# Seven half products for the last 256 tokens, and weight sums and loads put in other queues

## Chip, cores and metric

The kernel runs on one core of one Trainium2 chip. The metric is the device time of one execution in microseconds, as the median of several runs. Before the change it is 205.13 us (three runs, 204.55 to 205.29).

TensorE (PE) multiplies matrices into PSUM, VectorE (DVE), ScalarE (ACT) and GpSimd (POOL) work element by element, and SyncE (SP) issues most of the DMAs. Each engine takes its instructions in the order in which the program lists them for it. They wait for one another through semaphores.

## The reference

The reference is a cross attention between tokens `x` (8 batches, 8 heads, 512 tokens, 64 wide) and a state of 32 tokens per head, followed by a two-layer network with SiLU:

```python
a = softmax(scale * x @ state.T);   xread = a @ state    # 512 tokens a batch
a2 = softmax(scale * state @ x.T);  sread = a2 @ x       # 32 tokens a batch
t = concatenate([xread, sread])     # heads side by side: 512 wide, 544 tokens a batch
h = t @ w_in                        # 512 -> 2048
out = (h * sigmoid(h)) @ w_out      # 2048 -> 512, float32
```

The 32 state-read tokens of all eight batches make 256 tokens, which the kernel treats as a ninth unit at the end.

## The kernel before the change

**Stages.** Batch 0 is written out by hand. Then comes a loop over batches b = 1 to 7 (line 858). For each, `emit_G1` (line 549) makes 16 tiles of 128 hidden features by 512 tokens: TensorE multiplies, ScalarE applies SiLU and writes the tile `g`. The attention of an x-read batch is folded into the weights: `W1[b]` (lines 462 to 493) is the state times `w_in`, and `aT[b]` holds the normalised weights of the attention. `upto(k)` (line 710) emits G1 tiles until k are done, so it places G1 work between other products. n = b + 1 and m = b + 2 name the batches prepared during batch b.

**Output product of a batch.** `class Unit` (line 608) does the output product in the manner of Strassen and Winograd: the 2048 features are cut in two halves of eight tiles, the 512 output columns in two halves of 256, and the 512 tokens in two halves of 256. Seven half products then stand in for eight. `mm` (line 623) numbers them 1 to 7. They need sums of the token tiles (`sums3`, `sums2`, `sums1`, `sums4`, on VectorE) and sums of weights, `D1` to `D4`, which `t_weights` (line 596) makes once. During batch 1, `D2` and `D4` are completed for their second half of the features by two VectorE sums (lines 936 and 972). Results are gathered in the two tiles `u.o[0]` and `u.o[1]` (tags `o_sb0` and `o_sb1`, one buffer each) and written by `out_half(1)` and `out_half(0)`.

**Order of the batch.** Within batch b the list is: G1 tiles from `lead` to 15 with products 1 and 7 between them (lines 884 to 912), then product 2, 6, 4, 5, 3 (lines 945 to 1009). At j = 5 the first `sums3` and, from batch 2 on, the next load of x; at j = 9 the second `sums3` and, in batches 1 and 2, `evict_state`, which places transposed states into `stT` (in batch 2 ahead of `norm_t`). In batch 1, lines 971 to 980 place `t_weights`, `spread_x`, the normalisation and transposes of batch 2's attention, `exps_t(m)` (it ends with a DMA transpose into `e`) and `fetch_x(m + 1)` (two loads of x of 512 KB each, from SyncE's queue). `cast_x` and `transpose_x` at the batch's end (lines 1010 to 1013) need that load.

**State-read tokens.** `emit_G1` makes 16 tiles of 256 tokens for them (lines 555 to 566), spread over batch 7's products. After batch 7, lines 1014 to 1022 do the output product directly: the first 128 tokens by 16 matmuls of 512 columns (`G2`, line 577), then `last_cols` (line 691) three times for the other 128 tokens: 256 columns, 128 and 128, 16 matmuls each, each followed by a copy to a buffer of its own and a DMA.

**Places that the change and the prediction touch.** `D2`, `D4` and `t_weights`: lines 586 to 606, 936, 972. `evict_state` in batch 2: line 903. `fetch_x` in batch 1: line 979. The sum that frees PSUM for product 3: line 989. `scores_t`, which reads `xT`: line 329. The tail: lines 1016 to 1022. Helpers: `copy` (160, 162), `sub` (591), `add` (594).

Of the kernel before, what the change touches and what calls it, by code (L numbers as in the profile page):

```python
# [8 lines left out]
FP32 = mybir.dt.float32  # L9
# [9 lines left out]
B = 8  # L19
# [23 lines left out]
def kernel(  # L43
# [33 lines left out]
    def bank(shape, dtype, name):  # L77
        tag = banks[turn[0] % len(banks)]
        turn[0] += 1
        return psA.tile(shape, dtype, tag=tag, name=name)  # L80
# [77 lines left out]
    def copy(eng, dst, src):  # L158
        if eng is nc.scalar:
            nc.scalar.activation(dst, src, func=COPY, bias=0.0)  # L160
        else:
            eng.tensor_copy(dst, src)  # L162
# [123 lines left out]
    def evict_state(u, eng, b0, nb):  # L286
        to = stT.rearrange("p b k s (n m v) -> p b k s n m v", n=2, m=8)
        for g in range(2):
            for v in range(2):
                copy(  # L290
                    eng,
                    to[ds(64 * u, 64), ds(b0, nb), ds(2 * g, 2), u ^ g, :, :, v],
                    st_x[
                        ds(64 * v, 64), :, ds(b0, nb), ds(2 * g, 2), u, :
                    ].rearrange("p m b k n -> p b k n m"),
                )
# [391 lines left out]
            nc.sync.dma_start(out_sread[ds(512, 32), ds(4 * tt, 4), :], o[:])  # L688


    def last_cols(b, tt, f, n, eng, queue):
        cols = ds(f, n)
        ps = bank([128, DM], FP32, "o_part")
        for ft in range(NFT):
            nc.tensor.matmul(  # L695
                ps[:, 0:n],
                gt[b * NFT + ft][:, ds(128 * tt, 128)],
                w_out_sb[:, ft, cols],
                start=(ft == 0),
                stop=(ft == NFT - 1),  # L700
                skip_group_check=True,
            )
        o = opool.tile([128, n], FP32, tag=f"o_part{f}", name="o_part")
        copy(eng, o[:], ps[:, 0:n])
        queue.dma_start(out_sread[ds(512, 32), ds(4 * tt, 4), cols], o[:])


    done = [0]

    def upto(k):  # L710
        while done[0] < min(k, (B + 1) * NFT):
            emit_G1(done[0])
            done[0] += 1
# [139 lines left out]
    def fetch_x(i):  # L853
        n = 4 if i < 6 else H
        for h in range(0, H, n):
            load_x(i, h, n, nc.sync)

    for b in range(1, B):
        n = b + 1
        m = n + 1  # L860
        u = Unit(b)
        lead = 3 if b == 1 else LEADS
        last = 6 if b == 1 else 8
        todo = [(1, k) for k in range(last)] + [(7, k) for k in range(8)]
        todo += [(1, k) for k in range(last, 8)]
        n_todo = len(todo)

        def unit():
            p, k = todo.pop(0)
            u.mm(p, k)  # L870
            if (p, k) == (1, 7):
                u.keep(nc.vector, 0, 0)
            if (p, k) == (7, 7):
                copy(nc.vector, u.block(1, 1), u.be[:])

        def early(j):
            while (
                todo
                and todo[0][1] + (0 if todo[0][0] == 1 else 2) <= j - 2
                and (n_todo - len(todo)) * (NFT - lead) < 16 * (j + 1 - lead)  # L880
            ):
                unit()

        for j in range(lead, NFT):
            upto(NFT * b + j + 1)
            if j == 8:
                u.hi = gh[b, 1]
            if j == max(lead, 5):
                if b == 1:
                    t_weights((3,), 4, 4)  # L890
                    transpose_x(3)
                u.sums3(0, 4)
                if 1 < b and m + 1 < B:
                    fetch_x(m + 1)
            if j == 9:
                u.sums3(4, 4)
                if b == 1:
                    for v in range(2):
                        evict_state(v, (nc.vector, nc.gpsimd)[v], 2, 2)
                elif n < B:  # L900
                    if b == 2:
                        for v in range(2):
                            evict_state(v, (nc.vector, nc.gpsimd)[v], 4, 4)
                    norm_t(n)
                    if b in SREAD_AT:
                        spread_x(n)
                else:
                    for half in range(2):
                        place_xm(half, nc.vector)
            early(j)  # L910
            if j == 13:
                u.sums2(0, 4)
        srs = SREAD_AT.get(b, ())

        def group_a():
            pss = w1_next(PIECES_A[b])
            if m < B:
                scores_t(m)
            ps_sr = sread(srs, bank if m < B else new_h) if srs else None
            return pss, ps_sr  # L920

        def out_a():
            w1_out(*made[0][0])
            if srs:
                sread_out(srs, made[1])
            for piece in made[0][1:]:
                w1_out(*piece)

        while todo:
            unit()  # L930
        u.sums2(4, 2)
        if 1 < b < B - 1:
            made = group_a()
        u.sums2(6, 2)
        if b == 1:
            t_weights((2,), 4, 4)
            u.sums1()
        if 1 < b < B - 1:
            out_a()
        if n == B:  # L940
            upto(NFT * B + 2)
        if b == 1:
            for hg in range(2):
                scores(2, hg)
        for k in range(8):
            u.mm(2, k)
        add(nc.vector, u.block(0, 0), u.block(0, 0), u.be[:])
        if b == 1:
            for hg in range(2):
                exps(2, hg)  # L950
        elif m < B:
            nc.scalar.activation(warm[:], busy[:, 0:1], func=EXP, bias=0.0)

        if 1 < b and m < B:
            exps_t(m)
        step = 0

        def units(p, leads={}):
            nonlocal step
            for k in range(8):  # L960
                u.mm(p, k)
                if n == B and (p != 6 or k > 5):
                    upto(NFT * B + 2 + (step + 1) * (NFT - 2) // 26)
                    step += 1
                if n < B and k in leads:
                    upto(NFT * n + leads[k])

        units(6)
        u.keep(nc.scalar, 1, 0)
        add(nc.gpsimd, u.block(1, 0), u.block(1, 0), u.block(1, 1))  # L970
        if b == 1:
            t_weights((4,), 4, 4)
            spread_x(2)
            for hg in range(2):
                norm(2, hg)
                transpose_a(2, hg)
            made = group_a()
            exps_t(m)
            fetch_x(m + 1)
            out_a()  # L980
        else:
            u.sums1()
            if n < B and b not in SREAD_AT:
                spread_x(n)
        if m < B:
            nc.scalar.activation(warm[:], busy[:, 0:1], func=SILU, bias=0.0)
        units(4)
        u.sums4()
        add(nc.vector, u.block(1, 0), u.block(1, 0), u.be[:])
        def group_b():  # L990
            if b in PIECES_B:
                c = PIECES_B[b]
                pss = w1_next(2) + (w1_next(1, new_h) if c == 3 else [])
                for i in (2, 0, 1)[3 - c :]:
                    if b == 1 and i == 1:
                        pss[i] = pss[i][:2] + ((nc.vector, nc.vector),) + pss[i][3:]
                    w1_out(*pss[i])

        if b > 1:
            group_b()  # L1000
        units(5, {7: 1} if b > 1 else {})
        u.keep(nc.scalar, 0, 1)
        add(nc.gpsimd, u.block(1, 1), u.block(1, 1), u.block(0, 1))
        u.out_half(1)
        if b == 1:
            group_b()
        units(3, {1: 2, 3: 3, 5: 4, 7: 5})
        add(nc.vector, u.block(0, 1), u.block(0, 1), u.be[:])
        u.out_half(0)
        if m + 1 < B:  # L1010
            for c in range(4):
                cast_x(m + 1, nc.gpsimd, c, 1)
            transpose_x(m + 1)
        for ft in range(NFT):
            gt.pop(NFT * b + ft)
    for ft in range(NFT):
        upto(NFT * B + ft + 2)
        G2(B, 0, ft)
    store(B, 0, nc.scalar)
    last_cols(B, 1, 0, 256, nc.scalar, nc.sync)  # L1020
    last_cols(B, 1, 256, 128, nc.vector, nc.scalar)
    last_cols(B, 1, 384, 128, nc.vector, nc.sync)
# [1 line left out]
_INS = ['x', 'state', 'moe_w_in', 'moe_w_out']  # L1024
_OUTS = [((4352, 512), 'float32')]
# [25 lines left out]
```

## Time and profile before

| what | value |
|---|---|
| median of three runs | 205.13 us |
| the profiled execution | 204.79 us |
| its span | 202.9 us |
| granted TensorE clock, mean | 0.998 |
| GpSimd busy | 68.2 us (34%) |
| DMA moved | 28.71 MB, mean 141 GB/s |

The span is the profiled part of the execution; 1.9 us lie around it. In a timeline row, the first figure is the start in us from the span's begin, the second the length of the group, then engine, line, operation, output and inputs with their shapes, and how many instructions were merged. Square brackets give the idle time of the engine ahead of the row and what ended it. That releaser is inferred: where several things were awaited, it is the one that came last by the profile, and a DMA can hide behind it. "PEld" is TensorE's loading of weights, which runs beside its matmuls. A DMA has two times: the length of its issue in a queue (SPq is SyncE's), and the time from the issue to its landing.

### The profile page before, as it was taken

How to read it: one execution, taken by the hardware profiler on the slowest of the kernel's cores; microseconds unless marked ns; L12 is line 12 of the kernel's file. 1: busy time of each engine (PE TensorE's matmuls, PEld its weight loads, DVE VectorE, ACT ScalarE, POOL GpSimd, SP SyncE). 2: the span in 40 equal slices, each digit the busy share in tenths (PEclk: the TensorE clock that was granted, in tenths of full speed). 3: DMA queues.
4: the chain of work that ended last, by engine and by line, in shares of the span. 5: the costliest groups of instructions: out<-in, count | busy, mean ns of one | idle time of the engine just before them, and what ended most of it. 6: DMA issues, size and time to landing. Idle time of an engine off the chain costs nothing.

```text
span 202.9 us, 4636 instructions
## 1 busy us (share of the span) xinstructions
PE 194.5 (96%) x1893; PEld 129.7 (64%) x1912; DVE 133.6 (66%) x237; ACT 137.5 (68%) x243; POOL 68.2 (34%) x87
## 2 busy tenths in 40 slices
PE   7799999999989989999999999999999999999993
PEld 2454445458756577667766677668766876688862
DVE  2852747958985999387947974779369955861101
ACT  2875667888767867889778957788588168724510
POOL 8682343850623703730373033332202230002200
PEclk9999999999999999999999999999999999999999
DMA  6999999992078992495229913944142005000222
GB/s 196 196 206 207 264 249 359 240 234 52 3 149 284 216 253 56 167 275 129 52 114 181 280 21 55 279 86 29 29 203 55 13 3 207 0 3 0 103 107 103
DMA packets 40965, 28.71 MB, mean 141 GB/s; under 512 B 27376, under 2 KB 37616, under 8 KB 40944
## 3 DMA queue, kind: packets, MB, share of 16 engines
q1 hardware_dynamic: 34736, 20.65, 39.9%
q0 software_dynamic: 5920, 7.64, 18.2%
q8 instruction: 15, 0.25, 0.5%
q10 hardware_dynamic: 288, 0.13, 0.3%
q14 instruction: 6, 0.05, 0.1%
HBM read 17.43 MB, written 8.91 MB: 130 GB/s over the span
## 4 chain that ended last, share of the span: by engine, by line
PE 87%; DVE 7%; DMA 2%; issue 1%; ACT 1%
PE o L642 40%; PE h L540 25%; PE o L577 5%; PE ps_w L473 4%; PE h L558 4%; PE o_a L577 3%; DMA x_f<-in_x_dram 2%; PE o_part L695 2%; DVE o_sb L162 1%; PE ps_xt L257 1%; PE ps_sr L420 1%; DVE s L591 1%; DVE g L591 1%; DVE W L162 1%; ACT xT L160 1%
## 5 line engine op out<-in xcount | busy, mean ns | idle before, releaser
L568 ACT ACTIVATE g<-h 128x512 bf16<-128x512 f32 (+1 forms) x142 | 79.9, 573 | 34.6 <-PE h L540 17.4
L642 PEld LDWEIGHTS <-g 128*128 128x128 bf16 x560 | 54.1, 98 | 30.2 <-issue 1.4
L540 PE MATMUL h<-aT,W 128*128 128x512 bf16 x237 | 69.5, 379 | 0.1
L642 PE MATMUL o<-w_out_sb,g 128*128 128x256 bf16 x336 | 48.7, 273 | 1.1 <-DVE o_sb L594 0.6
L594 POOL TENSOR_TENSOR o_sb<-o_sb 128x512 f32<-128x512 f32 x14 | 20.3, 1447 | 83.0 <-ACT o_sb L160 67.8
L642 PE MATMUL o<-wt,g 128*128 128x256 bf16 x224 | 33.1, 273 | 0.4
L594 DVE TENSOR_TENSOR o_sb<-o_sb,o 128x512 f32<-128x512 f32 x21 | 14.4, 684 | 28.0 <-PE o L642 26.7
L540 PEld LDWEIGHTS <-W 128*128 128x128 bf16 x252 | 24.4, 98 | 8.4 <-issue 0.6
L642 PE MATMUL o<-wt,s 128*128 128x256 bf16 x224 | 27.4, 273 | 0.0
L162 DVE CAST W<-ps_w 128x512 bf16<-128x512 f32 (+1 forms) x36 | 22.4, 664 | 5.9 <-PE ps_w L473 5.9
L642 PEld LDWEIGHTS <-s 128*128 128x128 bf16 x224 | 21.5, 98 | 4.2 <-issue 1.7
L160 ACT ACTIVATE o_sb<-o 128x512 f32<-128x512 f32 x16 | 9.5, 595 | 14.9 <-issue 8.1
L160 ACT ACTIVATE W<-ps_w 128x512 bf16<-128x512 f32 (+1 forms) x30 | 15.9, 582 | 5.1 <-PE ps_w L473 5.0
L162 POOL CAST x_nat<-x_f 128x512 bf16<-128x512 f32 x24 | 16.0, 709 | 6.7 <-DMA x_f<-in_x_dram 6.7
L591 DVE TENSOR_TENSOR g<-g 128x1024 bf16<-128x1024 bf16 x14 | 11.3, 804 | 9.5 <-ACT g L568 9.5
L162 DVE COPY o_sb<-o 128x512 f32<-128x512 f32 x15 | 10.3, 685 | 5.7 <-PE o L642 5.5
L591 DVE TENSOR_TENSOR g<-g,s 128x1024 bf16<-128x1024 bf16 x14 | 13.3, 991 | 0.0
L366 POOL TENSOR_TENSOR an<-e,rcn 128x512 bf16<-128x512 bf16 x5 | 7.7, 1540 | 16.4 <-DVE rcn L364 16.4
L577 PE MATMUL o<-w_out_sb,g 128*128 128x512 bf16 x46 | 12.9, 380 | 0.1
L577 PEld LDWEIGHTS <-g 128*128 128x128 bf16 x80 | 7.3, 98 | 8.7 <-issue 0.8
L591 DVE TENSOR_TENSOR s<-g 128x512 bf16<-128x512 bf16 (+1 forms) x21 | 10.8, 541 | 0.1
L473 PE MATMUL ps_w<-w_in_sb,stT 64*32 64x512 bf16 (+1 forms) x264 | 10.2, 375 | 0.0
(91 smaller groups left out, 184.2 us busy)
## 6 DMA issues: line engine op xcount, KB each, us to landing
out_dram<-o_sb SPq DMA_DIRECT2D x14, 512.0 KB, 2.7
x_f<-in_x_dram SPq DMA_DIRECT2D x6, 512.0 KB, 4.6
x_f<-in_x_dram POOLq DMA_DIRECT2D x2, 1024.0 KB, 11.4
x_f<-in_x_dram SPq DMA_DIRECT2D x2, 1024.0 KB, 6.0
w_out_sb<-in_moe_w_out_dram POOLq DMA_DIRECT2D x6, 256.0 KB, 10.8
w_in_sb<-in_moe_w_in_dram POOLq DMA_DIRECT2D x3, 512.0 KB, 10.5
out_dram<-o_sb SPq DMA_DIRECT2D x5, 256.0 KB, 5.3
x_f<-in_x_dram POOLq DMA_DIRECT2D x2, 512.0 KB, 15.1
```

The lines of the kernel that those rows point to most:

```text
L160: nc.scalar.activation(dst, src, func=COPY, bias=0.0)
L162: eng.tensor_copy(dst, src)
L366: eng.tensor_tensor(a[:, hg], e2[b][:, hg], rc[:, hg].to_broadcast([128, 4, 4, NS]), op=MULT)
L473: nc.tensor.matmul(pss[f, hg][ds(32 * s, 32), 0:n], stT[ds(r, 64), b, h // 2, s % 2, :], w_in_sb[ds(r, 64), h // 2, ds(f, n)], start=True, ...
L540: nc.tensor.matmul(h_ps[k][:], W1[b][:, hg, ds(128 * ft, 128)], aT[b][:, hg, :, :], start=(hg == 0), stop=(hg == 1), skip_group_check=True,)
L558: nc.tensor.matmul(ps[:, 0:256], w_in_sb[:, kt, ds(128 * ft, 128)], xmT[:, :, kt].rearrange("p t n b -> p t (n b)"), start=(kt == 0), stop ...
L568: nc.scalar.activation(gt[k], ps[:, 0:n], func=SILU, bias=0.0)
L577: nc.tensor.matmul(outs[tt][:], gt[b * NFT + ft][:, ds(128 * tt, 128)], w_out_sb[:, ft, :], start=(ft == 0), stop=(ft == NFT - 1), skip_gr ...
L591: eng.tensor_tensor(dst, a, c, op=SUB)
L594: eng.tensor_tensor(dst, a, c, op=ADD)
L642: nc.tensor.matmul(to[:, t, :], left[:, ds(128 * t, 128)], right[:, k, :], start=first and t == 0, stop=(k == 7), skip_group_check=True,)
L695: nc.tensor.matmul(ps[:, 0:n], gt[b * NFT + ft][:, ds(128 * tt, 128)], w_out_sb[:, ft, cols], start=(ft == 0), stop=(ft == NFT - 1), skip_ ...
```

## The change

Four things change.

1. In batch 1, the second halves of `D2` and `D4` are summed on GpSimd, in one place after its part of `evict_state`, and not on VectorE in two places.
2. In batch 2, `evict_state` for batches 4 to 7 stands at j = 5, after the first `sums3`, and not at j = 9 after the second.
3. In batch 1, `fetch_x(m + 1)` stands ahead of `exps_t(m)`.
4. The output product of the 256 state-read tokens is done by seven half products with two halves of 128 tokens. Product 3 is cut in two groups of 128 columns. The sum that the batches call `sums3` is made in batch 7, at product 3's second step (`sread_diff`). The result tiles use the tags `o_sb0` and `o_sb1`.

```diff
-    def last_cols(b, tt, f, n, eng, queue):
-        ...
+    def sread_out_product():
+        g = gh[B, 0]
+        half = lambda e, t: g[:, ds(8 * e, 8), ds(128 * t, 128)]
+        a11, a21, a12, a22 = half(0, 0), half(0, 1), half(1, 0), half(1, 1)
+        t8 = lambda nm: spool.tile([128, 8, 128], BF16, tag=nm, name=nm)
+        s1, s2 = t8("s1"), t8("s2")
+        u1, u3 = (spool.tile([128, 256], FP32, tag=nm, name=nm) for nm in ("u1", "u3"))
+        o = [opool.tile([128, DM], FP32, tag=f"o_sb{i}", name="o_sb") for i in range(2)]
+        al = psO.tile([128, 256], FP32, tag="o1", name="o")
+
+        def product(left, right, to=None, first=True, c=0, n=256):
+            if to is None:
+                to = bank([128, 256], FP32, "o_s")
+            for k in range(8):
+                nc.tensor.matmul(
+                    to[:, 0:n],
+                    left[:, k],
+                    right[:, k, ds(c, n)],
+                    start=(first and k == 0),
+                    stop=(k == 7),
+                    skip_group_check=True,
+                )
+            return to
+
+        def out(t, c, n, queue):
+            queue.dma_start(
+                out_sread[ds(512, 32), ds(4 * t, 4), ds(c, n)], o[t][:, ds(c, n)]
             )
+        lo, hi = ds(0, 256), ds(256, 256)
+        s3 = a21
+        product(a11, B11, al)
+        copy(nc.vector, o[0][:, lo], al[:])
+        for k0, n in ((0, 6), (6, 2)):
+            k = ds(k0, n)
+            sub(nc.vector, s2[:, k], a22[:, k], s3[:, k])
+        p7 = product(s3, D3)
+        copy(nc.scalar, o[1][:, hi], p7[:])
+        product(s2, D2, al, False)
+        add(nc.vector, s1[:], s2[:], a11)
+        copy(nc.scalar, u1[:], al[:])
+        p2 = product(a12, B21)
+        add(nc.vector, o[0][:, lo], o[0][:, lo], p2[:])
+        out(0, 0, 256, nc.sync)
+        sub(nc.vector, a12, a12, s2[:])
+        add(nc.vector, u1[:], u1[:], o[1][:, hi])
+        product(s1, D1, al, False)
+        copy(nc.scalar, u3[:], al[:])
+        add(nc.vector, o[1][:, hi], o[1][:, hi], u3[:])
+        p4 = product(a22, D4)
+        add(nc.vector, o[1][:, lo], u1[:], p4[:])
+        out(1, 0, 512, nc.sync)
+        for c, queue in ((0, nc.scalar), (128, nc.sync)):
+            p3 = product(a12, B22, c=c, n=128)
+            add(nc.vector, o[0][:, ds(256 + c, 128)], u3[:, ds(c, 128)], p3[:, 0:128])
+            out(0, 256 + c, 128, queue)
+
+    def sread_diff():
+        g = gh[B, 0]
+        sub(nc.vector, g[:, 0:8, 128:256], g[:, 0:8, 0:128], g[:, 0:8, 128:256])
...
                     fetch_x(m + 1)
+                if b == 2:
+                    for v in range(2):
+                        evict_state(v, (nc.vector, nc.gpsimd)[v], 4, 4)
             if j == 9:
...
                         evict_state(v, (nc.vector, nc.gpsimd)[v], 2, 2)
+                    t_weights((2, 4), 4, 4, nc.gpsimd)
                 elif n < B:
-                    if b == 2:
-                        for v in range(2):
-                            evict_state(v, (nc.vector, nc.gpsimd)[v], 4, 4)
                     norm_t(n)
...
         if b == 1:
-            t_weights((2,), 4, 4)
             u.sums1()
...
+                    if (p, k) == (3, 1):
+                        sread_diff()
...
-            t_weights((4,), 4, 4)
             spread_x(2)
...
+            fetch_x(m + 1)
             exps_t(m)
-            fetch_x(m + 1)
             out_a()
...
-    for ft in range(NFT):
-        upto(NFT * B + ft + 2)
-        G2(B, 0, ft)
-    store(B, 0, nc.scalar)
-    last_cols(B, 1, 0, 256, nc.scalar, nc.sync)
-    last_cols(B, 1, 256, 128, nc.vector, nc.scalar)
-    last_cols(B, 1, 384, 128, nc.vector, nc.sync)
+    upto(NFT * B + NFT)
+    sread_out_product()
```

More of the change, by code (lines that the diff above doesn't have):

```diff
@@ L688, in store @@
             nc.sync.dma_start(out_sread[ds(512, 32), ds(4 * tt, 4), :], o[:])
-    def last_cols(b, tt, f, n, eng, queue):
-        cols = ds(f, n)
-        ps = bank([128, DM], FP32, "o_part")
-        for ft in range(NFT):
[L695 to L701, printed above, removed]
-            )
-        o = opool.tile([128, n], FP32, tag=f"o_part{f}", name="o_part")
-        copy(eng, o[:], ps[:, 0:n])
-        queue.dma_start(out_sread[ds(512, 32), ds(4 * tt, 4), cols], o[:])
+    def sread_out_product():
[23 more added lines that the diff above has]
+                out_sread[ds(512, 32), ds(4 * t, 4), ds(c, n)], o[t][:, ds(c, n)]
+            )
+        lo, hi = ds(0, 256), ds(256, 256)
[25 more added lines that the diff above has]
+            out(0, 256 + c, 128, queue)
@@ L1015 @@
             gt.pop(NFT * b + ft)
-    for ft in range(NFT):
-        upto(NFT * B + ft + 2)
-        G2(B, 0, ft)
-    store(B, 0, nc.scalar)
-    last_cols(B, 1, 0, 256, nc.scalar, nc.sync)
-    last_cols(B, 1, 256, 128, nc.vector, nc.scalar)
-    last_cols(B, 1, 384, 128, nc.vector, nc.sync)
+    upto(NFT * B + NFT)
+    sread_out_product()
 _INS = ['x', 'state', 'moe_w_in', 'moe_w_out']
```

## The prediction

> **What bounds the kernel now.** I read the page's busy table first, then TensorE's waits, then the timeline around each wait and around the end.
>
> ```profile
> PE 194.5 (96%) x1893; PEld 129.7 (64%) x1912; DVE 133.6 (66%) x237; ACT 137.5 (68%) x243; POOL 68.2 (34%) x87
> ```
>
> TensorE is busy 96% of the span, so a change pays only by fewer matmul columns or by closing one of its few gaps. Its waits after the start-up are these (columns: total us, times, longest):
>
> ```profile
> PE ps_scT L336 <- DVE s L591: 0.8, 1, 0.8
> PE o L642 <- DVE o_sb L594: 0.6, 1, 0.6
> ...
> PE o L642 <- DVE o_sb L162: 0.2, 1, 0.2
> ```
>
> The 0.6 us stands in batch 1, at 58.00, ahead of product 3. The two others stand in batch 2, at 71.67 and 72.28. From there to 199.41 TensorE waits for nothing. Nothing later than 72.28 runs by an absolute time, so what is won there should arrive at the end.
>
> **The tail: arithmetic.** TensorE's timeline ends so:
>
> ```profile
> 192.26 3.62 PE L577 MATMUL o<-w_out_sb,g 128*128 128x512 bf16 x15
> 195.71 3.70 PE L695 MATMUL o_part<-w_out_sb,g 128*128 128x256 bf16 x48
> ```
>
> L577 runs 16 matmuls (one record is missing) of 512 columns from 192.26 to 195.71: 3.45/16 = 0.216 us each. Groups of 16 matmuls of 256 columns last 1.91 us (L642, at 49.61) and one matmul 0.273, so the step is (1.91 - 0.273)/15 = 0.109. L695 is 16 of 256 columns (1.75) and 32 of 128; its slots are about 3.70 - 0.15 = 3.55 (the last matmul's drain taken off, an estimate from 0.273 - 0.109), which leaves 1.80/32 = 0.0565 for 128 columns. Before: 3.45 + 3.55 = 7.00, slots end 199.26. After: 48 of 256 (5.24) and 16 of 128 (0.90) = 6.14. Taken alone the seven products save **0.86 us**.
>
> In a sentence apart: the Trainium skill, "TensorE: Matmul & The Clock Gate", section "Back-to-back issue gap", gives some 81 ns per matmul of 128 columns with its weight load. By it the last product's 16 would take 1.30 us, not 0.90, and its being cut in two groups of columns would cost 0.4. The row shows 56.5 ns, weight loads included, and I keep the row.
>
> **The tail: a new wait.** sread_out_product takes its result tiles from the tags o_sb0 and o_sb1, the buffers of batch 7's output; last_cols and o_one had buffers of their own. In the changed kernel's queue order the first VectorE instruction of the tail, the copy of product 1 into o[0], waits for the DMA of out_half(0) of batch 7. That DMA is issued late:
>
> ```profile
> 192.09 0.69 DVE L594 TENSOR_TENSOR o_sb<-o_sb,o 128x512 f32<-128x512 f32 x1 [6.73 <-PE o L642]
> ```
> ```profile
> 192.81 0.33 SPq L673 DMA_DIRECT2D out_dram<-o_sb  x1
> ```
> ```profile
> out_dram<-o_sb SPq DMA_DIRECT2D x1, 512.0 KB, 2.6
> ```
>
> The first is VectorE's last sum of batch 7, the second the issue behind it, the third (issues of 192 to 196) its time to landing. It lands at 192.81 + 2.6 = **195.4**. Product 1 is done at 193.3. Behind the held copy stand, on VectorE, the two subtractions that make s2, and product 6 needs s2: TensorE does products 1 and 7 (16 slots, to 194.01) and then stops, and since it takes its work in order products 2, 5, 4, 3 stop with it. Costs behind the landing: the copy, 128x256 out of PSUM, 0.42 (between 0.29 for 128 and 0.685 for 512 columns); the first subtraction, 768 elements, 0.55 (between 0.42 for 512 and 0.69 for 1024); signals and one weight load 0.1. That is 196.45, a stop of **2.45 us**. After it the chain is dense: s1 is done at 197.1, needed at 198.2; a12-s2 at 199.45, needed at 199.95; u1, u3 lie beside products on ScalarE (0.38 each). The slots end at 192.26 + 6.14 + 2.45 = 200.85 instead of 199.26: **+1.6**. The way from the last matmul to the span's end (one VectorE instruction of 0.29, an issue of 64 KB landing in 1.9) is as before. SyncE's issue ahead of it, of out(1), begins at 200.6 and takes 0.67, so it is over at 201.3, as the last sum ends. ScalarE's copy into o[1] waits for out_half(1), issued at 190.62 and landed at 193.2, before product 7 ends: no cost. The sum sread_diff (0.69) falls into VectorE's idle 6.73 us: nothing. Without the hold, copy and subtraction behind product 1 would still make product 6 wait 0.35.
>
> **Batch 1: two weight sums leave VectorE.** From 46.3 to 57.9 VectorE works without a gap and ends with the sum that product 3 waits for.
>
> ```profile
> 47.02 0.69 DVE L591 TENSOR_TENSOR s<-g 128x1024 bf16<-128x1024 bf16 x1
> 47.63 0.68 DVE L162 COPY o_sb<-o 128x512 f32<-128x512 f32 x1
> 48.23 0.75 DVE L591 TENSOR_TENSOR s<-g 128x512 bf16<-128x512 bf16 x2
> 48.90 0.68 DVE L591 TENSOR_TENSOR wt<-w_out_sb,wt 128x1024 bf16<-128x1024 bf16 x1
> ```
>
> The two wt sums take 0.60 of VectorE's time each; without them it ends 1.2 earlier. But GpSimd holds VectorE up while it sums. At 76.63:
>
> ```profile
> 76.63 2.36 DVE L591 TENSOR_TENSOR g<-g,s 128x1024 bf16<-128x1024 bf16 x2
> ```
> ```profile
> 76.69 1.75 POOL L594 TENSOR_TENSOR o_sb<-o_sb 128x512 f32<-128x512 f32 x1 [5.61 <-ACT o_sb L160]
> ```
>
> Two VectorE sums take 2.36 instead of 1.28: the first ends with GpSimd's instruction. No row has a GpSimd sum of 128x1024 bf16: two of its 128x512 bf16 (1.04 each, an) make 2.08, two of 128x512 float32 (1.265 at least) 2.53. I take 2.3, the middle. GpSimd is free at 43.40 (its stT copies), so the sums end at 48.0. D2 is needed at 50.5 and D4 at 53.9 by the fifth step of products 6 and 4: no wait. VectorE's sum at 47.02 however ends at 48.0 + 0.6 instead of 47.63: 1.0 lost of the 1.2. Bounds: at 2.08 each, 0.5 lost; at 2.53, 1.4, and if GpSimd first has to let VectorE's stT copies pass (to 43.94), 2.0. A cap stands at the other side: batch 2's second aT transpose, issued at 55.97, lands after 2.4, at 58.4, and the first G1 of batch 2 uses it at 58.66, so at most 0.25 is won unless GpSimd's normalisation ahead of it also comes earlier. I take a gain of **0.1** (from a loss of 0.8 to a gain of 0.55).
>
> The Trainium skill, "GPSIMD Engine Reference", section "3.1 Elementwise — side-by-side cycle accounting", has 2.6 cycles per element of a two-input sum, by which I estimate 2.2 us each and a gain here of 0.3; no run here shows it yet.
>
> **Batch 2: two gaps.** Releaser "DVE s" at 71.67 had long been done for that operand; what scT reads last is xT.
>
> ```profile
> 66.79 2.75 SPq L147 DMA_TRANSPOSE xT<-x_nat  x1
> ```
>
> With 4.7 to landing that is 71.5, just ahead of 71.67. The transpose waits for GpSimd's casts (63.98 to 66.76), and those for x_f, issued at 58.70 behind the e transpose. The change issues x_f first, 1.26 earlier, with no e transpose (1.5 us of DMA) ahead: casts from about 62, xT lands between 69.5 and 70.3. That removes 0.8. The e transpose moves behind x_f's megabyte and lands near 63.5; its reader comes at 66. The other 0.20 (72.28) waits for VectorE's copies; evict_state (2.19) moves into VectorE's idle 1.65 at 63, so norm_t and the copies behind it come about 2 earlier and the copy runs as product 7 ends. SyncE's other issues keep their order, and what is behind xT (the next x_f, aT) comes earlier. Gain **1.0** (0.5 if VectorE is held by the casts, 0 if xT is no earlier).
>
> **Sum.** Against the profiled execution, 204.79 (span 202.9 and 1.9 around it): +1.6 - 0.1 - 1.0 = +0.5, so 205.3. The median of the runs, 205.13, lies 0.34 above that execution; I say **205.4**.
>
> **Rivals.** (1) *No hold*: the buffer is let go earlier than 193.3, or the copy is not what s2 stands behind. Tail -0.86 + 0.35 = -0.5, batches -1.1: 203.2. Against it: the wait is in the queue, and the landing time has min and max of 2.5 and 2.7. Chance 0.13; that the products then save nothing is part of the forecast. (2) *GpSimd's sums cost more than they free* (slower): from 2.41 us each (43.40 + 2 x 2.41 + 0.6 = 47.63 + 1.2) VectorE reaches product 3 later than before, and each 0.1 more costs 0.2; the copy of product 1 that product 6 waits for (49.61) slips too. At 2.75 with the later start batch 1 loses 1.0 to 1.2: 206.5. For it: GpSimd's same sum ran 1.27 to 1.75. Chance 0.17. (3) *The clock drops* in the new stop. After the last matmul (199.41) the granted clock (the third figure from the right) goes:
>
> ```profile
> 201.80:202.00 0.20, 0.00 (x0) 1.00 0.00 0
> 202.00:202.20 0.20, 0.00 (x0) 0.90 0.00 0
> 202.20:202.40 0.20, 0.00 (x0) 0.50 0.00 0
> ```
>
> It halves 2.75 us after work ends; the stop, from 194.17 to 196.45, is 2.3. Halving for the rest of the stage would add at least 1.7: 207.0. Chance 0.09. The Trainium skill, "TensorE: Matmul & The Clock Gate", Part 1, speaks of a window of about 3.4 us that runs freely; by it a 2.3 us stop never fills one and costs nothing, while the row shows a drop after less than a whole idle window.
>
> **Chances and range.** Forecast 0.61, with its own range 204.3 to 206.2. Half a per cent is 1.03 us, about what a measurement of this kernel can tell from no change. Faster 0.13 (rival 1), same 0.61, slower 0.26 (rivals 2 and 3). The range 204.1 to 206.9 takes in the bounds of batches 1 and 2 and rival 2, and leaves out rival 1 and part of 3.
>
> **What would show it.** In the after profile: a stop of about 2.4 us on TensorE between L705's 16th and 17th matmuls, released by VectorE's s2, and ahead of it VectorE idle until a landing of out_dram; no gap at 71; at 58 a gap shorter or much as now; VectorE's first sum in batch 1 lengthened to over 1 us by GpSimd. A tail with no stop, or a gap at 71 still there, proves me wrong.

## The result, and the profile after

The changed kernel takes **207.59 us** (median of four executions, 207.05 to 211.83) against 204.90 before. The ratio is **1.0123**, with a 95% interval of [1.0096, 1.0150]: it is slower by 2.5 us. The forecast was 205.4, "same", with a range up to 206.9. Both the forecast of no change and the range missed.

The profiled execution took 207.05 (span 205.2, against 204.79 and 202.9 before). TensorE's waits in it (columns: total us, times, longest):

```profile
PE o L705 <- DVE s L591: 2.3, 1, 2.3
...
PE ps_scT L336 <- DMA xT<-x_nat: 1.0, 1, 1.0
...
PE o L642 <- DVE o_sb L594: 0.2, 1, 0.2
```

The first is new and stands in the tail. The second was 0.8 before (then put down to VectorE) and was to vanish. The third was 0.6 and stands at 58. VectorE's and TensorE's timelines in the tail:

```profile
195.84 0.42 DVE L162 COPY o_sb<-o 128x256 f32<-128x256 f32 x1 [2.75 <-DMA out_dram<-o_sb]
196.18 0.75 DVE L591 TENSOR_TENSOR s<-g 128x768 bf16<-128x768 bf16 x2
```
```profile
193.44 1.04 PE L705 MATMUL o_s<-wt,g 128*128 128x256 bf16 x8
196.78 1.05 PE L705 MATMUL o<-wt,s 128*128 128x256 bf16 x8 [2.31 <-DVE s L591]
```

VectorE sits idle for 2.75 us until batch 7's store lands, copies product 1, and only then makes s2; TensorE stops for 2.31 after product 7. The chain that ended last says the same, with a stretch in which nothing computes:

```profile
192.40 0.70 DVE o_sb L594
193.11 2.61 DMA out_dram<-o_sb
...
195.84 0.42 DVE o_sb L162
196.26 0.47 DVE s L591
...
196.78 1.05 PE o L705 x8
```

Where the 2.3 us between the two profiled spans lie: TensorE's last stage begins at 192.56 instead of 192.26 (+0.3, where 1.1 less was forecast from batches 1 and 2), and from there to the span's end it takes 12.64 instead of 10.64 (+2.0). This profile was 0.67 late at 47 us already, ahead of everything that was moved, so what batches 1 and 2 gained has to be read elsewhere (e4_batches below). Of the four executions two had a mean granted clock of 1.0 (207.05, 207.17) and one had 0.992 (208.02); the fourth (211.83, also at 0.992) is slower by another 3.8 us that no trace explains, and the ratio leaves it out.

### The profile page after: what moved, and what is told of

It is laid out like the page before. It is cut to its first block, busy times and chain, and to the rows that moved or that the text cites. A ratio compares the mean times of both kernels' runs of the same rounds, so it can differ in the third digit from the quotient of the medians.

```text
span 205.2 us, 4651 instructions
## 1 busy us (share of the span) xinstructions
PE 194.6 (95%) x1894; PEld 130.9 (64%) x1912; DVE 139.9 (68%) x245; ACT 137.7 (67%) x244; POOL 72.5 (35%) x89
## 4 chain that ended last, share of the span: by engine, by line
PE 76%; DMA 12%; DVE 7%; POOL 2%; issue 1%; ACT 0%; DVEq 0%; POOLq 0%
PE o L642 39%; PE h L540 21%; DMA x_f<-in_x_dram 7%; PE h L558 3%; DMA xT<-x_nat 3%; PE ps_w L473 3%; PE ps_busy L168 2%; PE o_a L577 2%; PE o_s L705 1%; DMA out_dram<-o_sb 1%; DVE o_sb L594 1%; PE ps_xt L257 1%; PE o L577 1%; PE o L705 1%; DVE rs L383 1%
## 5 line engine op out<-in xcount | busy, mean ns | idle before, releaser
L642 PEld LDWEIGHTS <-g 128*128 128x128 bf16 x560 | 54.1, 98 | 29.6 <-DVE g L591 0.7
L540 PE MATMUL h<-aT,W 128*128 128x512 bf16 x237 | 69.5, 379 | 0.1
L642 PE MATMUL o<-w_out_sb,g 128*128 128x256 bf16 x336 | 48.7, 273 | 0.5 <-DVE o_sb L594 0.2
L591 DVE TENSOR_TENSOR g<-g 128x1024 bf16<-128x1024 bf16 x15 | 11.8, 788 | 8.8 <-ACT g L568 8.8
L160 ACT ACTIVATE o_sb<-o 128x512 f32<-128x512 f32 x15 | 8.9, 595 | 11.7 <-issue 8.1
L162 DVE COPY o_sb<-o 128x512 f32<-128x512 f32 (+1 forms) x16 | 10.7, 670 | 8.0 <-PE o L642 3.6
L591 DVE TENSOR_TENSOR g<-g,s 128x1024 bf16<-128x1024 bf16 x15 | 14.0, 970 | 0.0
L591 DVE TENSOR_TENSOR s<-g 128x512 bf16<-128x512 bf16 (+3 forms) x23 | 12.0, 551 | 0.1
L577 PEld LDWEIGHTS <-g 128*128 128x128 bf16 x64 | 5.8, 98 | 7.0 <-issue 0.8
L577 PE MATMUL o_a<-w_out_sb,g 128*128 128x512 bf16 x31 | 9.8, 379 | 0.2
```

Of the source, the lines that this page charges most:

```text
L540: nc.tensor.matmul(h_ps[k][:], W1[b][:, hg, ds(128 * ft, 128)], aT[b][:, hg, :, :], start=(hg == 0), stop=(hg == 1), skip_group_check=True,)
L577: nc.tensor.matmul(outs[tt][:], gt[b * NFT + ft][:, ds(128 * tt, 128)], w_out_sb[:, ft, :], start=(ft == 0), stop=(ft == NFT - 1), skip_gr ...
L591: eng.tensor_tensor(dst, a, c, op=SUB)
L642: nc.tensor.matmul(to[:, t, :], left[:, ds(128 * t, 128)], right[:, k, :], start=first and t == 0, stop=(k == 7), skip_group_check=True,)
```

## The experiments

Each group ran on one chip with the kernel before beside it (204.7 to 204.8 us in each).

### What the tail's stop is made of

**Own buffers (e1_own).**

```diff
-        o = [opool.tile([128, DM], FP32, tag=f"o_sb{i}", name="o_sb") for i in range(2)]
+        o = [opool.tile([128, DM], FP32, tag=f"o_s{i}", name="o_sb") for i in range(2)]
```

> The changed kernel, with two result buffers of the tail's own in place of batch 7's. Theory H (the hold: the tail's first copy waits for batch 7's last store to land, and the two subtractions for product 6 stand behind it): VectorE starts that copy as product 1 ends, TensorE's 2.31 us stop shrinks to about 0.4, and the kernel takes 1.9 to 2.1 us less than the changed one. Rival D (the stop is product 6's need of s2, made so late by the order of the products): the stop stays at 2 us and the time at that of the changed kernel.

Measured: 205.21, ratio 1.0017 [0.9987, 1.0047] to before; 2.4 us below the changed kernel. The profiled execution was 2.7 us behind that of the kernel before at 50 us already, so only distances are read in it.

```profile
196.42 0.42 DVE L162 COPY o_sb<-o 128x256 f32<-128x256 f32 x1 [0.55 <-PE o L705]
```
```profile
196.22 1.04 PE L705 MATMUL o_s<-wt,g 128*128 128x256 bf16 x8
197.37 1.05 PE L705 MATMUL o<-wt,s 128*128 128x256 bf16 x8
```

The copy now waits for product 1 alone. Product 6 begins 1.15 us after product 7, where eight matmuls take 0.87: the stop is 0.28 (0.35 was worked out for a tail with no hold). From its first product to the span's end the tail takes 10.45, against 12.64 in the changed kernel. The hold is shown, rival D falls. But the old tail took 10.64: little of the 0.86 that the products save has arrived, and the time is that of the kernel before.

**The two buffers exchanged (e2_swap).** The edit is `tag=f"o_sb{1 - i}"`.

> The changed kernel with the tail's two result tiles exchanged between the two buffers, so that VectorE's first copy needs the buffer whose store was issued 2.2 us earlier, and ScalarE's copy of product 7 needs the late one. Theory H: no stop before product 6 beyond 0.4 us; ScalarE's copy waits to about 195.8 and pushes the copy to u1 behind it, so that TensorE stops about 0.5 us before product 5 instead; tail 1.3 to 1.6 us shorter than in the changed kernel. Rival D: the stop before product 6 stays.

Measured: 205.59 in a single execution; its tail takes 10.57, so 2.1 less than the changed kernel's, where 1.3 to 1.6 was expected. Product 6 follows product 7 after 1.17 us, so its stop is 0.3. ScalarE, which now holds the late buffer, waits:

```profile
196.50 0.38 ACT L160 ACTIVATE o_sb<-o_s 128x256 f32<-128x256 f32 x1 [2.68 <-DMA out_dram<-o_sb]
196.78 0.38 ACT L160 ACTIVATE u<-o 128x256 f32<-128x256 f32 x1
```

The wait moved with the buffer, and product 5 came 1.05 after product 2 instead of 0.87: a stop of 0.18, where 0.5 was expected. The same wait costs 2.3 us on one engine and 0.2 on another, by what is queued behind it.

**The tail alone (e3_tail).** The kernel before, with `sread_out_product` and `sread_diff` as in the changed kernel, and nothing moved in batches 1 and 2.

> The kernel before with the new tail alone, nothing moved in batches 1 and 2. Theory H: 1.6 us more by TensorE's stop and 0.4 more by the later landing of the last stores, 2.0 us over the kernel before. If the queue changes of batches 1 and 2 cost something of their own (theory Q), this one is clearly below the changed kernel; if they gain what batch 1's shorter gap shows (0.4), it is 0.3 to 0.5 above it.

Measured: 208.35 (206.51 to 208.68), ratio 1.0154 [1.0109, 1.0199]. The four executions fall in two kinds: 206.51 with a mean clock of 1.0, and 208.26, 208.44 and 208.68 with 0.992. The profiled one is of the second kind. By stretches of 1 us (columns: stretch, length, TensorE's busy time and matmuls, granted clock, DMA share, GB/s):

```profile
196.00:197.00 1.00, 0.10 (x1) 1.00 0.00 0
197.00:198.00 1.00, 1.00 (x6) 0.51 0.00 0
198.00:199.00 1.00, 1.00 (x7) 0.50 0.07 16
199.00:200.00 1.00, 1.00 (x7) 0.50 0.00 0
200.00:201.00 1.00, 1.00 (x9) 0.79 0.00 0
201.00:202.00 1.00, 1.00 (x12) 1.00 0.00 0
```

TensorE stopped from 194.58 to 196.90. At 197.0, just as product 6 begins, the clock halves, and it comes back at about 200.4. Product 6 takes 1.60 and product 2 takes 1.71, where 0.87 each is the rule: 1.6 us in all. So the stop costs its own 2.3 us in each execution, and some 1.6 more in those in which the clock drops. Expected were 2.0 over the kernel before; the execution at the full clock lies 1.7 over it and the others 3.4 to 3.9. With the clock in between, this run doesn't decide theory Q; e4_batches does.

**The stop filled with work (e10_fill).** The changed kernel, with ten matmuls of zeros ahead of product 6:

```diff
         copy(nc.scalar, o[1][:, hi], p7[:])
+        keep_busy(10, psH, "h1")
         product(s2, D2, al, False)
```

> The changed kernel with ten matmuls of zeros between products 7 and 6, so that TensorE has work during its stop of 2.3 us. Theory C (the stop itself halves TensorE's clock in some executions, for one window of about 3.4 us, and that is the difference between the changed kernel's executions of 207.1 and of 208.0 to 208.7): the granted clock stays at 1.0 in every execution, no execution lies at 208 or above, and the time is the 207.1 of the changed kernel's better executions, since the ten matmuls (2.2 us) end as product 6 may begin. Rival S (the scatter is of the start-up loads): executions of 208 and more stay.

Measured: 206.99 (206.58 to 208.08 in ten executions), ratio 1.0108 [1.0079, 1.0137]. No execution has a mean clock under 0.996. Theory C is borne out in the clock: 0.992 stood in two of the changed kernel's four executions, in three of four with the tail alone, and in none of ten here. One execution of 208.08 at a clock of 0.998 is left, against the expectation, so the small part of the scatter that the kernel before also shows (up to 207.19 at a clock of 0.999 in that group) is not of the clock. The median agrees with the changed kernel's executions at the full clock.

### What became of batches 1 and 2

**The queue changes alone (e4_batches).** The kernel before with changes 1 to 3, and the old tail.

> The kernel before with the queue changes of batches 1 and 2 alone and the old tail. If the 0.67 us by which the changed kernel's profile is already late at 46 us, ahead of everything that was changed, is chance of the start-up loads: 0.2 to 0.5 us less than before (batch 1's gap shortened by 0.4, batch 2's gap at product 2 unchanged since xT lands as late as before). Theory Q (the queue changes, or the program's changed code, cost time): 0.3 us or more above before, with the same lateness at 46 us.

Measured: 204.84, ratio 1.0014 [0.9991, 1.0038]: no difference. Theory Q falls, and so does the expected gain of 0.2 to 0.5. The 0.67 us by which the changed kernel's profile is late at 46 us is not there (VectorE's copy at 46.08 against 46.30 before), so that was start-up. Two things show why nothing is won. First, batch 1:

```profile
43.76 4.41 POOL L591 TENSOR_TENSOR wt<-w_out_sb,wt 128x1024 bf16<-128x1024 bf16 x2
```
```profile
46.81 1.90 DVE L591 TENSOR_TENSOR s<-g 128x1024 bf16<-128x1024 bf16 x1
```
```profile
57.79 0.60 PE L642 MATMUL o<-w_out_sb,g 128*128 128x256 bf16 x4 [0.55 <-DVE o_sb L594]
```

GpSimd's two sums last to 48.2, and VectorE's sum, which takes 0.69 by itself, ends only 0.5 behind them, at 48.7: 1.2 lost for 1.2 freed, and the gap at 58 is 0.55 as before. (In the changed kernel's profile, late at the start, less of that sum fell beside GpSimd's, it took 1.40, and the gap was 0.17.) Second, batch 2. The issue of the transpose and TensorE's wait for it:

```profile
65.13 4.68 SPq L147 DMA_TRANSPOSE xT<-x_nat  x1
```
```profile
PE ps_scT L336 <- DMA xT<-x_nat: 1.2, 1, 1.2
```

The transpose is issued 1.66 us earlier than before (66.79) but takes 6.7 to land instead of 4.7: 71.8 against 71.5. The 0.20 at 72.28 is gone, as forecast.

**Batch 1's stores left out (e5_nostore).** The same, with `out_half` skipped for b = 1.

> The queue changes of batches 1 and 2 with the old tail, and batch 1's two stores left out, so that the rows of batch 1 are not written. Theory F (the transpose into xT stands behind the stores' 1 MB in the DMA queue): xT lands by 70.3, some 1.5 us earlier than with the stores, the gap ahead of the state scores at 71 disappears and the kernel gains up to 1.0 us. Rival X (the transpose itself takes 6.7 us at that place): xT lands at about 71.8 as with the stores, and the gap of 1.2 us stays.

Measured: 203.91 in a single execution. The transpose is issued at 65.97 and lands after 4.0 us, at 70.0, and the wait for xT is gone. Theory F is borne out: behind 1 MB of stores an earlier issue does not land earlier. The other profiles say the same: in the nine kernels that issue the stores where the kernel before does (e1_own, disturbed, left out), xT lands 7.8 to 8.1 us after the first of the two stores is issued, whether its own issue follows that store after 1.1 us (e4_batches) or after 4.0 (e3_tail). Whether the transpose waits its turn in the queue or shares the DMA engines with the stores is not separated.

**The weight sums in an idle stretch of VectorE (e6_early).** The kernel before, with both sums of t_weights((2, 4), 4, 4) moved behind the transposes of batch 1's second half.

> The kernel before with the two sums of D2 and D4 still on VectorE, but made at 31.5 us, in an idle stretch, and not in batch 1. Theory L (in the changed kernel GpSimd's sums hold VectorE up by as much as they free): without them at either place VectorE ends its work for product 3 some 1.0 us earlier and the gap of 0.56 at 58 goes; of that up to 0.3 is taken again by the transpose into aT, so 0.2 to 0.5 us less than before. Rival P (the gap has another cause, such as the aT transpose or PSUM): the gap stays at 0.5.

Measured: 204.92, ratio 0.9995 [0.9966, 1.0024]. The gap at 58 is gone, as theory L has it, and rival P falls. But the time does not move, which neither theory had foreseen: TensorE's wait for xT is 1.17 us now, where 0.80 and 0.20 stood. The chain to xT passes by the gap at 58. It runs over GpSimd's work from 52.6 on and then, from 54.9, over SyncE's queue, which issues the transposes into aT and e, the loads of x and the transposes into xs with no pause above 0.2 us, and only then, at 63.98, the stores that xT lands behind. Closing the gap moves none of that: in this profile, 0.34 late at 47 us already, the stores go 0.29 later than before and xT lands 0.4 later. So what TensorE wins at 58, it waits out at 71.

### A version that works

**The tail without its waits.** A first trial (e8_order, on the kernel before) had own buffers and product 2 ahead of product 6.

> The kernel before in batches 1 and 2, with the new tail on buffers of its own and product 2 ahead of product 6. Theory H: no stop in the tail at all (product 6 starts 0.9 us later than s2 needs), so the 0.86 us of saved columns arrive, less the 0.4 of the later landing: 0.4 to 0.6 us less than before. If TensorE's columns in the tail are not what its end hangs on (rival E), the time stays at that of before.

Measured: 204.99, ratio 1.0019 [0.9979, 1.0059]; expected was a gain of 0.4 to 0.6. Product 6 has no stop, but product 5 has one:

```profile
196.42 1.03 PE L705 MATMUL o<-wt,s 128*128 128x256 bf16 x8 [0.47 <-ACT u L160]
```

Product 2 had covered ScalarE's copy of u1 out of the sum that product 5 goes on with; moved ahead, it covers it no more. The next trial (e12_tail) puts product 4 there:

```diff
         p7 = product(s3, D3)
         copy(nc.scalar, o[1][:, hi], p7[:])
+        p2 = product(a12, B21)
         product(s2, D2, al, False)
         add(nc.vector, s1[:], s2[:], a11)
         copy(nc.scalar, u1[:], al[:])
-        p2 = product(a12, B21)
...
+        p4 = product(a22, D4)
         add(nc.vector, u1[:], u1[:], o[1][:, hi])
+        add(nc.vector, o[1][:, lo], u1[:], p4[:])
+        out(1, 0, 256, nc.sync)
         product(s1, D1, al, False)
         copy(nc.scalar, u3[:], al[:])
         add(nc.vector, o[1][:, hi], o[1][:, hi], u3[:])
-        p4 = product(a22, D4)
-        add(nc.vector, o[1][:, lo], u1[:], p4[:])
-        out(1, 0, 512, nc.sync)
+        out(1, 256, 256, nc.sync)
```

> The kernel before in batches 1 and 2; the new tail on its own buffers, in the order of products 1, 7, 2, 6, 4, 5, 3, with the second token half's result written in two stores. Theory H (the tail's loss is its waits alone: the hold, then in the former trial 0.47 us for ScalarE's copy of u1 ahead of product 5, and 0.3 us by the later landing behind a store of 256 KB): no stop on TensorE in the tail, the last VectorE sum 0.7 to 0.9 us earlier against the tail's start than before, and 0.4 to 0.9 us less than before. Rival E (the end hangs on the stores): TensorE's part shortens and the time stays within 0.3.

Measured: 204.07, ratio 0.9966 [0.9953, 0.9979], 0.7 us less than before. All seven products follow one another at 0.87. The interval reaches from 0.4 to 1.0 us less, so this gain is clear of the noise, and rival E falls.

**The queue of batch 1.** In e11_bat the weight sums stand as in e6_early, loads and evictions as in the changed kernel, and the three transposes into xs of batch 1 go behind the one into xT:

```diff
-        for i, b in enumerate(bs):
-            nc.sync.dma_start_transpose(xs[:, b, :], xm[:, i].rearrange("p g d -> p (g d)"))
+        def to_xs():
+            for i, b in enumerate(bs):
+                nc.sync.dma_start_transpose(xs[:, b, :], xm[:, i].rearrange("p g d -> p (g d)"))
+
+        if bs[0] == 0:
+            late.append(to_xs)
+        else:
+            to_xs()
...
             transpose_x(m + 1)
+        while late:
+            late.pop()()
```

> The old tail; the loads and evictions of batches 1 and 2 as in the changed kernel, the two weight sums on VectorE at 31.5 us, and batch 1's three transposes into xs put behind the one into xT in SyncE's queue, so that the stores of batch 1 and xT go out earlier. Theory F (xT is late since its queue and its stores are): xT lands by 70, the gaps at 58 and at 71 both go, 0.8 to 1.4 us less than before. Rival G (what one gap gives, the other takes, whatever the queue does): within 0.3 us of before.

Measured: 204.22, ratio 0.9969 [0.9936, 1.0001]: 0.6 us less by the medians, at the edge of the noise, and less than the 0.8 to 1.4 expected. Neither gap is left. xT is issued at 66.65 and lands after 3.7, at 70.35: the stores now go at 61.3 and 62.6 and have landed by 67.1, where in the kernel before the second landed at 69.7. Which of the three parts does it was not tried singly; the weight sums alone (e6_early) and the loads and evictions with the sums on GpSimd (e4_batches) gained nothing.

**Both together (e9_best).**

> Both of the others together. If the two parts are independent, since TensorE works without a gap between them, the sum of their gains: 1.2 to 2.2 us less than before, and 3.5 to 4.5 us less than the changed kernel.

Measured: **202.94** (202.75 to 203.52), ratio **0.9913** [0.9897, 0.9929]: 1.9 us less than before and 4.6 less than the changed kernel. From 9 us to the end TensorE waits for nothing. The two parts' gains by their medians, 0.8 and 0.6, make 1.4 where 1.9 came; the difference is within the interval of e11_bat. The profile splits the 1.8 us between the spans: batch 2's product 2 (72.28 before) begins at 71.00, 1.28 earlier, the tail begins at 191.00 instead of 192.26, still 1.26 earlier, and takes 10.10 instead of 10.64.

## Why the prediction was wrong, point by point

- **The tail's arithmetic** ("alone the seven products save 0.86 us") was right: in e12_tail, with no stop, VectorE's last sum ends 6.68 after the tail's first matmul instead of 7.48, so 0.8 less. The 128-column matmuls run at 56 ns (16 take 1.06, one alone 0.219), so the figure of the profile's row was the one to keep.
- **The tail's new wait** was right in its mechanism and size. The landing was put at 195.4 with the stage beginning at 192.26; it came at 195.7 with 192.56. The stop was put at 2.45 and measured 2.47 from the slot of product 7's end (194.31) to 196.78. e1_own and e2_swap show that it is the buffer.
- **The way from the last matmul to the span's end**, put down "as before", was longer by 0.4: from VectorE's last sum's end the span lasts 3.53 instead of 3.16. The last 64 KB land after 2.2 instead of 1.9, right behind the store of 256 KB. With that store split (e12_tail) they land after 2.0, but the span still lasts 3.44 from the sum: their issue now leaves SyncE's queue 0.26 after the sum instead of 0.02, behind the issue of the added store.
- **Rival 3, the clock**, had a chance of 0.09 and stood outside the sum; it came in five of eight executions of the changed kernel and e3_tail. The step that failed is the comparison of 2.3 us of stop with the 2.75 us that passed at the kernel's end before the clock fell. That one figure is no threshold: after the last matmul the clock fell 2.5 us later in e1_own's profile and 3.7 later in the changed kernel's. The price per event (1.7 put down, 1.6 measured) was right. The Trainium skill, "TensorE: Matmul & The Clock Gate", Part 1, gives a window of about 3.4 us that runs freely and says that one idle window halves the clock. The length agrees (half clock from 197.0 to 200.4); that a whole window must be idle does not: 2.3 us without a matmul were enough here.
- **Batch 1** ("a gain of 0.1"): the size was right (0.0), and its working too. GpSimd's sums were put at 2.3 each and took 2.2. That agrees with the prediction's estimate of 2.2 from the 2.6 cycles an element in the Trainium skill's "GPSIMD Engine Reference", section 3.1. Missing was that a gain there could not have arrived: e6_early closes the gap, and the wait for xT takes it.
- **Batch 2** ("Gain 1.0") is the step that put the sum wrong by most. "xT lands between 69.5 and 70.3" took 4.7 from issue to landing for a constant. That is the time of an issue that comes 2.1 us after the stores' issues end; issued 0.3 behind them, the transpose took 6.5 and landed at 72.2, 7.8 after the first store, as before. The text had noted the stores only among the issues that "keep their order". Of the gain only the 0.20 came, and the longer wait for xT took that too.
- **"Nothing later than 72.28 runs by an absolute time"** was right, and e9_best shows it: 1.28 us won there, and 1.26 of it still there where the tail begins.

The sum again, with what the runs show: +2.0 for the tail, 0 for batches 1 and 2, and 1.6 in about half of the executions. That is 206.9 at the full clock (207.0 in e10_fill) and 208.5 with the drop, and the median of 207.59 lies between the two kinds. Against the forecast of 205.4 the batches make 1.1, the way behind the last matmul 0.4, and the clock the rest.

## What to carry to other kernels

A buffer taken from a pool at the end of a kernel brings the last store of its former owner with it: ask of each tile that a change renames when its last reader, a DMA too, lets it go, and what is queued behind the first instruction that writes it. A DMA that is issued earlier in a queue lands earlier only if nothing large stands in front of it, so follow the bytes and not the issue. And where a later wait comes by a chain that passes by the place where time is won, the time is lost again there: both must go, or neither is worth anything.

## What the runs showed of the hardware

- With one stop of 2.3 us on TensorE, 2 of 4 and 3 of 4 executions of two kernels had a mean granted clock of 0.992; the trace of one shows it halved for 3.4 us from the stop's end. With zeros multiplied in the stop none of 10 was under 0.996.
- A GpSimd sum of two 128x1024 bf16 tensors takes 2.2 us (4.41 for two). A VectorE sum in SBUF beside it ended only 0.5 after it (1.90 instead of 0.69). VectorE's copies of SBUF data near it were longer in some profiles: the four stT copies took 3.07 in the changed kernel's and 4.78 in e5_nostore's, against 1.21 in e4_batches' and 1.11 before.
- One DMA transpose of 512 KB landed 4.0 us after its issue with no stores ahead of it (e5_nostore), 3.7 when the stores had been issued 4 to 5 us ahead and were nearly through (e11_bat), and 6.5 to 6.7 when issued 0.1 to 0.3 behind 1 MB of stores; its issue on SyncE lasted 1.6 us in e11_bat and 4.7 in e4_batches.
